# Attention's chunk loop: the state's update is recorded in front of the read-out of the old state

## The chip, the cores and the metric

The program runs on one core of a Trainium2 chip. TensorE (PE, its weight loads are listed apart as PEld), VectorE (DVE), ScalarE (ACT), GpSimd (POOL) and SyncE (SP, which here only starts DMAs) each work through an instruction list of their own and wait for each other through semaphores. The metric is the device time of one execution in microseconds.

## The reference

Three steps follow one another: a recurrent attention, a mixture of eight experts, and a dense layer pair with a squared ReLU. Only the first is touched. For each of 4 x 8 heads a 40 x 40 state is carried over 768 tokens:

```
y[t]  = r[t] . state                                  (read before the update)
Sa    = state . a[t]
state = state * w[t]  -  Sa x b[t]  +  v[t] x k[t]    (outer products)
```

The output of the whole program is `_moe2_ref(_moe_ref(attention))`, 3072 rows of 320 numbers.

## The kernel before

The 768 tokens are cut into 24 chunks of 32. For a chunk the decay is folded into scaled inputs, the 32 x 32 triangular system inside the chunk is inverted, and the state is carried from chunk to chunk in two PSUM tiles, ST0 and ST1. A chunk's work is cut into stages (functions A_... to F_...), and the table ORDER lists the stages of one loop iteration with a lag: `("D_st", 0)` in iteration i works on chunk i, `("E_yi", -1)` on chunk i-1, `("D_R", 1)` on chunk i+1. The loop runs over i = 1 to 21 (`for i in range(1, nch - 2)`); HEAD and TAIL are tables for the chunks before and after. Nothing reorders the work later: within `tc.manual_schedule()` every engine's list is what the stages issue, in the table's order, so each engine's order follows from the table.

Stages that matter here, with their lines:

- E_yi (L732): 16 matmuls that read the old state out for chunk i-1, `y = r . Ss`, where Ss is a transposed copy of the state in SBUF made an iteration earlier. They take a fresh buffer of the PSUM pool psm, which has six buffers in turn.
- D_st (L659, L676): 32 short matmuls add chunk i's contribution to ST0 and ST1, and four ACT copies bring the new state into SBUF (sT). At a window's end (i = 11 inside the loop) DVE rescales the state on the way (L674), followed by filler matmuls (DMY, L328) and matmuls that put the rescaled state back into ST (L682).
- D_R (L622, L629): the right-hand side of chunk i+1. Its first part (L622) needs no state; its second part (L629) reads sT, the copies that D_st of the same iteration has just made.
- E_scm (L723, DVE) masks a score matrix; E_y (L743, PE) multiplies it and adds to the y that E_yi began; E_xs (L771, DVE), the first DVE work of the next iteration, reads the finished y.
- C_inv, C_dn, C_x1, F_2, B_ev and the two scans (L752 and L446) fill DVE's list between L771 and the next L723. B_ev (L509, L513) reads the PSUM tile LM that PE fills at L500.
- loadE, loadL and loadV, loadZ of the next iteration are DMAs that SP starts in this order. loadL (L435, L439) refills xL, the tile whose first part E_yi reads as r, so SP holds it until E_yi is done.

The trace shows each fp32 matmul of the code as two records: the 16 matmuls of E_yi are "x32", the 32 of D_st are "x64".

```
P.matmul(y[32*b : 32*b+32, 2*hp : 2*hp+2], s["r"][:, hp*4+b], s["Ss"][:, hp*4+b], start=(hp == 0), stop=False, ...)   # E_yi, L732
P.matmul(ST[bl][64*hh : 64*hh+40, o : o+40], s["kS"][:, bl, hp, bh, hh], z[:, bh, hp, 40*hh : 40*hh+40], ...)         # D_st, L659
S_.activation(dst, src, AF.Copy)                                                                                     # D_st, L676
P.matmul(R[32*hp : 32*hp+32, b], s["at"][:, hp*4+b], cur[0:NP, hp*4+b], start=False, stop=True, ...)                  # D_R, L629
```

Of the kernel before, what the change touches and what calls it, by code (L numbers as in the profile page):

```python
# [72 lines left out]
def layout(r, k, v, w, a, b, moe_w_gate, moe_w_output_gate, moe_w1, moe_w2, moe2_w_in, moe2_w_out):  # L73
# [65 lines left out]
    ("loadZ", 1),  # L139
    ("B_kt", 2, 1),  # L140
    ("F_3", -2),
    ("E_yi", -1),
    ("loadE", 4),
    ("D_st", 0),
    ("E_W", 0),
    ("A_bd", 3),
    ("loadL", 1),
# [1381 lines left out]
```

## Time and profile before

| | |
|---|---|
| median of 3 runs | 1040.94 us (1035.12 to 1048.4) |
| the profiled execution | 1040.41 us, span 1038.6 us |
| busy in the span | PE 944.7 us (91%), DVE 683.0 (66%), ACT 610.8 (59%), POOL 463.6 (45%) |
| attention's loop | about 78 to 402 us of the span |
| experts and dense layers | about 440 to 1038 us |
| TensorE's granted clock, mean | 0.964 of full speed |

Times within the trace count from the span's start. A row of the timeline gives the start, the length and the number of instructions of a merged group; in brackets stands how long the engine had been idle before it and what ended the wait. "issue" is idle time in which the engine waited for nothing that the profile shows. A row of the waits gives the engine and line that waited, the one waited for, the total in us, the number of times and the longest.

### The profile page before, as it was taken

Reading aid. Unit: us, or ns where it says so; the run is one execution under the profiler, and the core shown is the slowest. Engines: PE = TensorE matmul, PEld = TensorE weight load, DVE = VectorE, ACT = ScalarE, POOL = GpSimd, SP = SyncE. Lnnn points to the kernel's source line nnn. Section 1 sums busy time; section 2 is a strip of 40 time slices with the busy share of each in tenths; the row PEclk is TensorE's granted clock in tenths of the full one; section 3 lists DMA queues with packets and bytes.
Section 4 is the critical chain, followed back from the end, with each engine's and each line's share of the span. In section 5 each row is a group of like instructions: output and inputs, shape, how many; then the busy total and the mean of one; then the engine's idle time right before and its main releaser. Section 6 shows DMA issues by size and latency. Waiting matters only on the chain.

```text
span 1038.6 us, 33215 instructions
## 1 busy us (share of the span) xinstructions
PE 944.7 (91%) x13882; PEld 835.9 (80%) x13882; DVE 683.0 (66%) x1752; ACT 610.8 (59%) x1366; POOL 463.6 (45%) x449
## 2 busy tenths in 40 slices
PE   1779889888889988889999999989999999999997
PEld 1568777777777776789999999978899998889986
DVE  5878899889988986537777777565443343434341
ACT  3569799896888987635555555544434344333432
POOL 5655777776676872527666666520100101010101
PEclk9779999999999999779999999999999999999999
DMA  4873445434344534356888876762001010000000
GB/s 100 247 206 107 114 107 138 124 108 115 107 116 109 144 91 116 111 207 193 246 245 252 245 231 199 214 139 64 29 13 32 26 31 27 1 26 1 17 10 26
DMA packets 59314, 120.33 MB, mean 116 GB/s; under 512 B 14609, under 2 KB 32145, under 8 KB 57233
## 3 DMA queue, kind: packets, MB, share of 16 engines
q1 hardware_dynamic: 51424, 103.09, 35.9%
q0 software_dynamic: 2688, 8.88, 2.4%
q10 hardware_dynamic: 5040, 6.12, 1.7%
q8 instruction: 112, 1.84, 0.8%
q14 instruction: 50, 0.40, 0.1%
HBM read 92.01 MB, written 26.05 MB: 114 GB/s over the span
## 4 chain that ended last, share of the span: by engine, by line
PE 51%; DMA 2%; DVE 1%; issue 1%; ACT 0%; POOLq 0%; POOL 0%; ACTq 0%; DVEq 0%; SPq 0%
PE ph L1226 26%; PE py L1409 9%; PE po L1230 5%; PE po L1229 5%; PE po L1231 5%; PE pk L1276 1%; DMA out_dram<-o,TID 1%; DMA q<-in_wo_dram 1%; DMA yTD<-yT 1%; DMA xg<-yTD 0%; DVE c L1211 0%; DVE c L1194 0%; PE py L1318 0%; POOLq L1524 0%; ACT r L1454 0%
## 5 line engine op out<-in xcount | busy, mean ns | idle before, releaser
L1226 PE MATMUL ph<-x,ring 128*128 128x512 f32 (+2 forms) x1344 | 308.1, 378 | 4.5 <-ACT r L1454 4.5
L1226 PEld LDWEIGHTS ph<-x,ring 128*128 128x128 f32 x1344 | 240.2, 189 | 38.6 <-ACT r L1454 5.0
L1480 POOL DMA_INDIRECT out_dram<-o,TID x24 | 27.9, 1163 | 323.4 <-ACT o L1478 279.5
L1455 DVE TENSOR_TENSOR q<-r 128x512 f32<-128x512 f32 x96 | 66.4, 691 | 122.5 <-ACT r L1454 122.5
L921 POOL TENSOR_TENSOR ring<-raws,ring 128x732 fp32r<-128x732 f32 (+2 forms) x72 | 123.3, 1726 | 48.1 <-ACT ring L920 28.1
L1454 ACT ACTIVATE r<-ph 128x512 f32<-128x512 f32 x96 | 57.3, 597 | 124.4 <-PE ph L1226 124.4
L486 POOL TENSOR_TENSOR arena<-arena 40x1024 f32<-40x1024 f32 x43 | 105.5, 2453 | 37.6 <-DVE arena L468 13.3
L1229 PE MATMUL po<-ring,hh 128*128 128x320 f32 x368 | 114.2, 310 | 0.0
L1230 PE MATMUL po<-ring,hl 128*128 128x320 f32 x368 | 114.1, 310 | 0.0
L1231 PE MATMUL po<-ring,hh 128*128 128x320 f32 x368 | 113.9, 309 | 0.0
L1409 PE MATMUL py<-hw,ring 128*128 128x448 f32 x512 | 106.1, 367 | 0.0
L1457 DVE TENSOR_TENSOR hl<-q,hh 128x512 fp32r<-128x512 f32 x92 | 63.8, 693 | 64.1 <-ACT hh L1456 64.1
L1409 PEld LDWEIGHTS py<-hw,ring 128*128 128x128 f32 x512 | 95.5, 188 | 7.9
L1456 ACT ACTIVATE hh<-q 128x512 fp32r<-128x512 f32 x92 | 58.1, 632 | 70.1 <-DVE q L1455 70.1
L1304 DVE SCALAR_TENSOR_TENSOR hw<-ph,hw 128x448 fp32r<-128x448 f32 (+2 forms) x72 | 41.0, 570 | 51.6 <-ACT hw L1303 51.6
L1229 PEld LDWEIGHTS po<-ring,hh 128*128 128x128 f32 x368 | 69.6, 189 | 4.3
L1230 PEld LDWEIGHTS po<-ring,hl 128*128 128x128 f32 x368 | 69.4, 189 | 3.9
L1231 PEld LDWEIGHTS po<-ring,hh 128*128 128x128 f32 x368 | 69.3, 188 | 0.0
L920 ACT ACTIVATE ring<-raws 128x732 fp32r<-128x732 f32 (+2 forms) x72 | 56.8, 790 | 4.8 <-DMA raws<-in_we_dram 4.2
L1303 ACT ACTIVATE hw<-ph 128x448 fp32r<-128x448 f32 (+2 forms) x72 | 36.1, 501 | 38.0 <-PE ph L1226 37.7
L1198 POOL TENSOR_TENSOR c<-c,r 128x384 int32<-128x384 int32 (+1 forms) x32 | 35.1, 1098 | 49.5 <-ACT yT L1414 12.0
L676 ACT ACTIVATE sT<-ST 40x320 f32<-40x320 f32 x88 | 33.2, 425 | 34.3 <-PE ST L659 34.1
(214 smaller groups left out, 1982.8 us busy)
## 6 DMA issues: line engine op xcount, KB each, us to landing
raws<-in_we_dram SPq DMA_DIRECT2D x48, 366.0 KB
arena<-in_xE_dram SPq DMA_DIRECT2D x48, 322.5 KB
xL<-in_xL_dram SPq DMA_DIRECT2D x24, 480.0 KB
xsD<-raws SPq DMA_DIRECT2D x24, 268.0 KB
q<-in_wi_dram SPq DMA_DIRECT2D x16, 384.0 KB
xg<-xsD SPq DMA_DIRECT2D x7, 804.0 KB
q<-in_wo_dram SPq DMA_DIRECT2D x16, 320.0 KB
wb<-in_wB_dram SPq DMA_DIRECT2D x24, 165.0 KB
```

The costliest lines, as they stand in the source:

```text
L486: (V if c < EARLY[2 + hh] else G).tensor_tensor(out=bd[sl, :, :, hh].rearrange("p a b c l j->p (a b) c (l j)"), in0=s["bk"][sl].rearrange( ...
L920: S_.activation(hi, rw, AF.Copy)
L921: G.tensor_tensor(out=lo, in0=rw, in1=hi.bitcast(F32), op=ALU.subtract)
L1226: P.matmul(ps, t[:, o : o + 128], x3[:, i, c], start=(j == 0), stop=(j == 7))
L1229: P.matmul(ps, hh, whi[:, o : o + 320], start=start, stop=False)
L1230: P.matmul(ps, hl, whi[:, o : o + 320], start=False, stop=False)
L1231: P.matmul(ps, hh, wlo[:, o : o + 320], start=False, stop=stop)
L1409: P.matmul(py, w, x, start=(f == 0 and k == 0), stop=last)
L1454: S_.activation(r, ph, AF.Relu)
L1455: V.tensor_tensor(out=q, in0=r, in1=r, op=ALU.mult)
L1456: S_.activation(hh, q, AF.Copy)
L1457: V.tensor_tensor(out=hl, in0=q, in1=hh.bitcast(F32), op=ALU.subtract)
```

## The change

In ORDER the row of E_yi moves behind the row of D_st. loadE (DMAs on SP) stood between them. HEAD and TAIL stay as they are.

```
--- before.py
+++ after.py
@@ -139,9 +139,9 @@
     ("loadZ", 1),
     ("B_kt", 2, 1),
     ("F_3", -2),
-    ("E_yi", -1),
     ("loadE", 4),
     ("D_st", 0),
+    ("E_yi", -1),
     ("E_W", 0),
     ("A_bd", 3),
     ("loadL", 1),
```

E_yi issues only matmuls, and in iteration 1 it issues none (chunk 0 has no old state), so the move shows in PE's list of 20 iterations; the lists of DVE, ACT, POOL and SP are the same in both kernels.

The first place is PE's list where the two stages stand, before, from the ranking matmul of the router (L895, tile rk) to the first update matmuls:

```order
L895 MATMUL rk<-oh,cnt 128x8 [waits DVE_49,PE_49,Activation_49]
L895 MATMUL rk<-oh,cnt 128x8
L732 MATMUL y<-Ss,xL_111 32x80 [waits DVE_49,PE_49]
L732 MATMUL y<-Ss,xL_111 32x80 x15
L659 MATMUL ST_108<-zS_117,kSB_121 40x40 [waits DMAHW2_49]
L659 MATMUL ST_108<-zS_117,kSB_121 40x40
L659 MATMUL ST_109<-zS_117,kSB_121 40x40 x2
```

The same place of an iteration in the changed kernel, from the last update matmuls to the right-hand side R:

```order
L659 MATMUL ST_108<-zS_118,kSB_124 40x40 x2
L659 MATMUL ST_109<-zS_118,kSB_124 40x40 x2
L732 MATMUL y<-Ss,xL_110 32x80 [waits DVE_49,PE_49]
L732 MATMUL y<-Ss,xL_110 32x80 x15
L622 MATMUL R<-vBD_119,MTm 32x4x40 [waits DMAHW6_49,DMAHW1_49,DMAHW7_49,DMAHW0_49,Activation_49]
L622 MATMUL R<-vBD_119,MTm 32x4x40 x7
L629 MATMUL R<-sT_115,at 32x80 [waits Activation_49]
L629 MATMUL R<-sT_115,at 32x80 x3
```

The update now follows L895 directly, and the read-out, with the wait for its buffer, stands between the update and R. L629's wait for ACT (the copies of the new state) is unchanged.

The second place is SP's list, which is the same in both kernels; it is shown for what loadL (xL, wb) waits for and what stands behind it:

```order
L416 DMA arena<-in_xE_dram 40x2064 [waits DMAHW2_49,Pool_49]
L435 DMA xL_110<-in_xL_dram 80x1536 [waits DMAHW3_49,PE_49]
L439 DMA wb<-in_wB_dram 128x330 [waits DMAHW4_49,DVE_49,Activation_49]
L423 DMA vBD_120<-in_vN_dram 32x320 [waits DMAHW5_49]
L423 DMA vBD_120<-in_vN_dram 32x320 [waits DMAHW6_49]
```

The row of xL waits for PE, and that is for the read-out E_yi, which now ends later in PE's list than before; wb and the four transfers of vBD stand behind it.

## Rows read from the trace of the kernel before

**Rows 1.** Busy time by stretch: length, then each engine, granted clock, DMA share, GB/s.

```profile
core 0: us, PE busy (x) PEld busy (x) DVE busy (x) ACT busy (x) POOL busy (x), PEclk, DMA share, GB/s
100.00:200.00 100.00, 88.12 (x2814) 74.46 (x2812) 89.78 (x307) 85.98 (x224) 72.47 (x80) 0.98 0.45 119
```

**Rows 2.** Waits from 85 to 405 us: who waited, for whom, total, times, longest.

```profile
DVE xs L771 <- PE y L743: 21.8, 17, 3.1
...
PE R L629 <- ACT sT L676: 10.0, 19, 0.7
...
PE y L743 <- issue: 7.6, 13, 2.1
PE y L732 <- DVE arena L513: 7.1, 10, 1.2
```

**Rows 3.** Timeline of PE in iteration 7: start, length, instructions, idle before.

```profile
168.81 0.36 PE L895 MATMUL rk<-oh,cnt 128*128 128x8 f32 x2
169.76 0.76 PE L732 MATMUL y<-Ss,xL 80*32 80x80 f32 x32 [0.58 <-DVE arena L513]
170.45 1.43 PE L659 MATMUL ST<-zS,kSB 128*40 128x40 f32 x64
171.80 0.75 PE L622 MATMUL R<-vBD,MTm 128*32 128x160 f32 x16
173.09 0.95 PE L629 MATMUL R<-sT,at 104*32 104x80 f32 x32 [0.54 <-ACT sT L676]
173.85 0.32 PE L743 MATMUL y<-kSB,scm 128*32 128x40 f32 x13
174.34 0.73 PE L743 MATMUL y<-kSB,scm 128*32 128x40 f32 x51 [0.17 <-issue]
```

**Rows 4.** Timeline of DVE in the same iteration.

```profile
168.94 0.67 DVE L513 STREAM_TRANSPOSE arena<-LM 128x512 f32<-128x512 f32 x1
...
172.46 0.67 DVE L723 TENSOR_TENSOR scm<-sc,cst 128x512 f32<-128x512 f32 x1
173.06 1.28 DVE L446 TENSOR_TENSOR_SCAN Cx<-arena 104x528 f32<-104x528 f32 x1
175.11 0.49 DVE L771 TENSOR_TENSOR xs<-y,WN 128x320 f32<-128x320 f32 x1 [0.77 <-PE y L743]
```

**Rows 5.** Timeline of ACT in the same iteration.

```profile
169.58 0.94 ACT L546 ACTIVATE kSB<-kt,cst 128x320 f32<-128x320 f32 x2
171.84 1.52 ACT L676 ACTIVATE sT<-ST 40x320 f32<-40x320 f32 x4 [1.33 <-PE ST L659]
```

**Rows 6.** DVE's groups by line, 85 to 405 us: busy, mean ns, idle before.

```profile
L771 DVE TENSOR_TENSOR xs<-y,WN 128x320 f32<-128x320 f32 x20 | 9.8, 488 | 22.8 <-PE y L743 21.8 <-PE tp L696 1.0
```

**Rows 7.** DVE at the window's end, iteration 11.

```profile
234.89 1.80 DVE L674 TENSOR_TENSOR sT<-ST,cw 40x320 f32<-40x320 f32 x4 [1.03 <-PE ST L659]
```

**Rows 8.** Timeline of PE at the window's end, iteration 11.

```profile
240.98 0.80 PE L743 MATMUL y<-kSB,scm 128*32 128x40 f32 x64 [0.78 <-DVE dB L765]
```

**Rows 9.** Waits of SP's queue, 85 to 405 us.

```profile
SPq L435 <- PE y L732: 127.5, 20, 8.5
```

**Rows 10.** PE's unexplained idle in E_y, iteration 15.

```profile
308.66 0.42 PE L743 MATMUL y<-kSB,scm 128*32 128x40 f32 x24 [2.12 <-issue]
```

**Rows 11.** DMA queue that carries instructions: packets, MB, share.

```profile
q8 instruction: 112, 1.84, 0.8%
```

**Rows 12.** PE's unexplained idle behind E_y, iteration 8.

```profile
192.47 0.60 PE L706 MATMUL zt<-cst,zS 128*80 128x128 f32 x4 [1.20 <-issue]
```

**Rows 13.** DVE afterwards, in iteration 9's first half.

```profile
197.63 0.16 DVE L876 TENSOR_REDUCE mx<-xs 128x1 f32<-128x8 f32 x1 [0.73 <-ACT xs L874]
...
198.99 1.25 DVE L509 STREAM_TRANSPOSE LB<-LM 128x1024 f32<-128x1024 f32 x1 [0.39 <-PE LM L500]
```

**Rows 14.** Busy time by stretch behind the loop, columns as in rows 1.

```profile
470.00:650.00 180.00, 180.00 (x929) 165.92 (x928) 137.18 (x260) 100.73 (x205) 116.68 (x80) 1.00 0.78 229
650.00:685.00 35.00, 30.47 (x146) 27.07 (x145) 21.87 (x41) 16.68 (x33) 20.86 (x14) 1.00 0.68 180
```

More of the change, by code (lines that the diff above doesn't have):

```diff
@@ L141 @@
     ("F_3", -2),
-    ("E_yi", -1),
     ("loadE", 4),
     ("D_st", 0),
+    ("E_yi", -1),
     ("E_W", 0),
```

## The prediction

> **What bounds the kernel now.** I read the busy times by stretch first. In attention's loop PE is busy 88% of the time, DVE 90%, ACT 86% [rows 1]: no engine is full, two run nearly level, so an iteration is set by where these two wait for each other. The waits of the loop show where. DVE's largest wait for PE is at L771, the first work on a finished y: 21.8 us in 17 iterations [rows 2], and with one more releaser 22.8 us over 20 iterations, about 1.1 us each [rows 6]. PE's two semaphore waits in the stretch that ends with that y are L629 for the copies of the new state (10.0 us, 19 times) and L732 for its buffer (7.1 us, 10 times) [rows 2]. The timelines of iteration 7 put them in one line: L732 starts 0.58 us late because DVE's L513 must first release a buffer, then come the update (L659), R's first part (L622), 0.54 us of waiting for ACT's copies, L629 and E_y (L743) [rows 3]; DVE has then been idle 0.77 us when it starts L771 at 175.11 [rows 4].
>
> **The change part by part.** Nothing is added or removed: 20 read-outs and 20 updates swap places on PE. The four ACT copies (L676) don't move in ACT's list, nor does SP's list change.
>
> *The wait for the copies.* The update now follows L895, which ends at 168.81 + 0.36 = 169.17 [rows 3]. It takes 1.43 us, so it ends at 170.6 instead of 171.88. ACT must be free then: its previous work L546 ends at 169.58 + 0.94 = 170.52 [rows 5], and it has idled 1.33 us before L676 in this iteration, so it is. L629 started 1.21 us behind the end of the update (173.09 against 171.88) and so may start at 171.8. On PE the read-out (0.69 us to the next start) and L622 (0.75 us) now stand between and end at 172.0. They cover the copies with 0.2 us to spare; the 0.54 us go.
>
> *The wait for the buffer.* L513 ends at 169.61 [rows 4], while the update runs; the read-out now asks for the buffer at 170.5. Those 0.58 us go as well.
>
> *What is late next.* L629 would be through at 172.7, but E_y needs L723's mask, which DVE ends at 172.46 + 0.67 = 173.13 [rows 4]. E_y starts there instead of at 173.85: 0.7 us won. It ends at 174.35, and DVE's L446 ends at 173.06 + 1.28 = 174.34, so L771 finds its input at once. In such an iteration the two engines meet, and 0.7 us is all there is.
>
> *The sum.* Of the 10 iterations with the buffer wait one is the window's end; the other 9 have both waits: 9 x 0.7 = 6.3 us. The 10 others have the wait for the copies alone, 0.54 us; in one of them DVE does not wait for PE (18 of 20 do [rows 2, 6], and the other exception is the window's end): 9 x 0.54 = 4.9 us. At the window's end DVE waits 1.03 us for the update itself [rows 7], and the update comes about as much earlier; the read-out then stands behind the rescaling, where its 0.7 us fit into the 0.78 us that E_y waits for DVE anyway [rows 8]: 1.0 us. Together 12.2 us. The largest it could be is DVE's whole waiting, 22.8 + 1.0 = 23.8 us.
>
> *What may be given back.* E_y also holds 7.6 us of idle in 13 pieces that no semaphore explains [rows 2], up to 2.12 us [rows 10]. There is a queue that carries only instructions, 112 packets of 16 KB [rows 11]; I take these pieces to be PE waiting for its own instructions. If such a piece ends at the same moment however early PE arrives, 0.54 us are lost there: at most 13 x 0.54 = 7.0 us, at least nothing. Most pieces are short (0.17 us in iteration 7 [rows 3], the mean is 0.58), so I take back 2 us, nearer the lower end. The Trainium skill ("Runtime: NRT & Kernel Launch", section "Instruction fetch mechanics") says instructions come in blocks of 16 KiB and that crossing into the next is mostly hidden; by that the sum would stay 12.2. The packet size agrees [rows 11]; "hidden" does not fit the 2.12 us [rows 10], if they are what I take them for.
>
> *SP.* loadL waits for the read-out 20 times [rows 9]. It now starts later by the update's 1.35 us (170.45 to 171.80 [rows 3]) less the buffer wait, and wb and vBD behind it too. They serve the next chunk, whose first use of them is a whole iteration away, and I cost the delay itself at nothing.
>
> *Behind the loop* PE is busy 100% of the 180 us from 470 on, and the 35 us behind them hang on work that PE releases [rows 14]. A shorter loop should shift all of it.
>
> 12.2 - 2 = 10.2 us off the profiled execution's 1040.41 gives **1030.2 us**. The median of the runs is 0.5 us above that execution, which I leave out.
>
> **Rivals.**
>
> *Nothing is given back.* For it: the short pieces may not be instruction waits at all. 1040.4 - 12.2 = 1028.2 us. The rule of the Trainium skill named above ("Runtime: NRT & Kernel Launch", "Instruction fetch mechanics") would give this time.
>
> *PE is held by its instructions.* For it: from L895 to the end of E_y there are 210 matmul records in 6.3 us [rows 3], and the unexplained idle sits at their end. All 13 pieces grow by what is won: 12.2 - 7.0 = 5.2 us, 1035.2 us; if iterations that have no such piece get one, or the 35 us behind the loop are set by DMA, it goes to no gain, 1040.
>
> *The idle in E_y goes too.* The xL transfer, which starts where the read-out ends, now starts nearer to E_y's end; if instruction packets have queued behind it during the update, they no longer do. 12.2 + 7.6 = 19.8 us, 1020.6 us.
>
> *Slower.* The same transfers (xL, wb, vBD) now run beside R, E_y and the transposes behind it, and the instruction wait moves there. It is not free: 1.20 us of it in iteration 8 [rows 12] was followed by DVE waits of 0.73 and 0.39 us [rows 13], 1.12 us in all. A gain of 0.6 us per iteration is eaten once each iteration gets 0.7 us of new idle there. At 1.20 us in all 20: 20 x 1.12 - 12.2 = 10 us slower, 1050.6 us; at 2.12 us about 1069. Against it: DMA is busy only 45% in the loop [rows 1].
>
> That the move does nothing (the update waiting for z or kS where the read-out stood) would need a wait that L659 never shows among the loop's waits although it starts at most about 1 us earlier; I count it into the no-gain end.
>
> **How the numbers follow.** Chances: the forecast (1026 to 1034) 0.45, nothing given back 0.13, held by instructions 0.20, the idle goes too 0.10, slower 0.12. The range 1020 to 1041 leaves out half of the tenth and most of the slower case. A change of 2%, 20.8 us, is about what a measurement of this kernel can tell from none. Below 1020.1 lies only the part of the fourth case in which nearly all of DVE's waiting goes: 0.05. Above 1061.8 only the slower case with the longest idle everywhere: 0.02. Within 2%: 0.93.
>
> **What would show it.** In the profile of the changed kernel L629's wait for ACT and L732's for L513 should be gone or near zero, and L743 should wait for DVE instead, 0.2 to 0.5 us per iteration. L771's 22.8 us should fall to about 12. From one L771 to the next it should be about 0.5 us less on average. If L743's unexplained idle is larger than 7.6 us, PE is held by its instructions; if it moved to L706, L696 or L607 and DVE waits more at L876 and L509, the transfers moved it. The prediction is wrong if L629 still waits, if the loop shortens without the end moving, or if the loop gets longer.

## The result and the profile after

The changed kernel takes **1029.17 us** (median of 6 runs, 1026.09 to 1034.66) beside 1040.93 us of the kernel before in the same series (6 runs, 1035.12 to 1048.4). The ratio is **0.990, 95% interval 0.986 to 0.994**. Run again, as the first of the experiments, it gave 0.994 (0.990 to 0.998). Ratios leave out executions more than 1.5% above the fastest of their kernel, so they can differ from the ratio of the medians. The prediction was 1030.2 us, and the medians came within 1 us of it.

The profiled execution of the change is the slowest of its six, 1034.66 us (span 1032.9). Its waits in attention's loop, 83 to 402 us, columns as in [rows 2]:

```profile
DVE xs L771 <- PE y L743: 8.3, 7, 2.3
...
PE y L743 <- issue: 5.4, 6, 1.6
...
DVE mx L876 <- ACT xs L874: 4.9, 5, 2.0
...
PE y L743 <- DVE scm L723: 3.6, 8, 0.8
```

PE's wait at L629 for the copies (10.0 us before) and L732's for DVE's L513 (7.1 us) have no row left. L743 waits for the mask instead, as was expected. Iteration 7 on PE, DVE and ACT, beside [rows 3 to 5]:

```profile
170.11 0.36 PE L895 MATMUL rk<-oh,cnt 128*128 128x8 f32 x2
170.41 1.43 PE L659 MATMUL ST<-zS,kSB 128*40 128x40 f32 x64
171.76 0.76 PE L732 MATMUL y<-Ss,xL 80*32 80x80 f32 x32
172.34 0.73 PE L622 MATMUL R<-vBD,MTm 128*32 128x160 f32 x16
173.05 0.94 PE L629 MATMUL R<-sT,at 104*32 104x80 f32 x32
174.38 1.09 PE L743 MATMUL y<-kSB,scm 128*32 128x40 f32 x64 [0.39 <-DVE scm L723]
```

```profile
173.65 0.68 DVE L723 TENSOR_TENSOR scm<-sc,cst 128x512 f32<-128x512 f32 x1
174.24 1.28 DVE L446 TENSOR_TENSOR_SCAN Cx<-arena 104x528 f32<-104x528 f32 x1
175.52 0.49 DVE L771 TENSOR_TENSOR xs<-y,WN 128x320 f32<-128x320 f32 x1
```

```profile
171.80 1.52 ACT L676 ACTIVATE sT<-ST 40x320 f32<-40x320 f32 x4
```

The first copy starts as the update ends, and L629 follows L622 without a wait: read-out and L622 cover the copies. E_y waits 0.39 us for the mask, and DVE goes from L446 to L771 without idling. From L895's start to E_y's end it is 5.36 us instead of 6.26. DVE's groups, 83 to 402 us, at L771 and at the window's end (beside [rows 6, 7]):

```profile
L771 DVE TENSOR_TENSOR xs<-y,WN 128x320 f32<-128x320 f32 x20 | 9.5, 475 | 8.4 <-PE y L743 8.3
...
L674 DVE TENSOR_TENSOR sT<-ST,cw 40x320 f32<-40x320 f32 x4 | 1.8, 484 | 0.0
```

L771's idle fell from 22.8 to 8.4 us, and L674's 1.03 us are gone. The whole loop, from the first L771 (iteration 1) to the 21st, columns as in [rows 1]: the kernel before, the change, and the second execution of the change (1028.12 us):

```profile
78.77:401.78 323.01, 288.99 (x9061) 245.60 (x9061) 287.57 (x983) 274.94 (x710) 227.50 (x256) 0.98 0.43 114
```

```profile
76.36:394.06 317.70, 289.81 (x9061) 248.87 (x9062) 294.53 (x983) 276.82 (x710) 229.03 (x256) 0.97 0.43 114
```

```profile
76.42:387.52 311.10, 285.24 (x9061) 244.04 (x9061) 289.67 (x984) 278.57 (x712) 228.60 (x256) 1.00 0.44 117
```

DVE's busy time is 287.57, 294.53 and 289.67 us. Its idle time (length less busy) goes from 35.4 to 23.2 and 21.4 us. But its busy time, for the same work, rises by 7.0 and 2.1 us, so the loop is only 5.3 and 11.9 us shorter. Where DVE's own time grows is the first open question; the second is why the two executions differ by 6.6 us. Outside the loop two differences nearly cancel. Its first L771 starts 2.4 us earlier than before (76.36 and 76.42 us instead of 78.77), where the lists are still the same, so that is not the change's. From the 21st L771 to the end it takes 638.8 us in both instead of 636.8.

DVE's groups for two small instructions of the router, 76 to 402 us, first before, then the change:

```profile
L878 DVE SCALAR_TENSOR_TENSOR val<-xs,mx,cst 128x8 f32<-128x8 f32 x20 | 8.3, 413 | 0.7
...
L882 DVE TENSOR_SCALAR oh<-val,mv 128x8 fp32r<-128x8 f32 x20 | 5.9, 295 | 0.7
```

```profile
L882 DVE TENSOR_SCALAR oh<-val,mv 128x8 fp32r<-128x8 f32 x20 | 12.2, 611 | 0.7
...
L878 DVE SCALAR_TENSOR_TENSOR val<-xs,mx,cst 128x8 f32<-128x8 f32 x20 | 10.8, 538 | 0.7
```

Together 14.2 us before and 23.0 after. One iteration of the change, DVE and then POOL:

```profile
182.16 0.59 DVE L878 SCALAR_TENSOR_TENSOR val<-xs,mx,cst 128x8 f32<-128x8 f32 x1
182.78 0.16 DVE L880 TENSOR_REDUCE mv<-val 128x1 f32<-128x8 f32 x1
182.98 1.05 DVE L882 TENSOR_SCALAR oh<-val,mv 128x8 fp32r<-128x8 f32 x1
```

```profile
180.36 2.36 POOL L486 TENSOR_TENSOR arena<-arena 40x1024 f32<-40x1024 f32 x1 [2.65 <-DVE ST L570]
182.80 1.20 POOL L473 TENSOR_TENSOR at<-arena,Cx 104x512 f32<-104x512 f32 x1
183.96 1.18 POOL L463 TENSOR_TENSOR arena<-Cx,arena 104x512 f32<-104x512 f32 x1
```

L878 ends when POOL's L486 does, and L882, 0.23 us elsewhere, ends when L473 does. L882 takes over 0.5 us 2 times in 20 before and 11 times in this execution of the change: a DVE that arrives earlier meets POOL's products.

### The profile page after: what moved, and what is told of

It is laid out like the page before. It is cut to its first block, busy times and chain, and to the rows that moved or that the text cites. A ratio compares the mean times of both kernels' runs of the same rounds, so it can differ in the third digit from the quotient of the medians.

```text
span 1032.9 us, 33234 instructions
## 1 busy us (share of the span) xinstructions
PE 945.0 (91%) x13882; PEld 838.3 (81%) x13882; DVE 688.8 (67%) x1752; ACT 611.9 (59%) x1366; POOL 465.9 (45%) x449
## 4 chain that ended last, share of the span: by engine, by line
PE 52%; DMA 2%; DVE 1%; issue 1%; ACT 0%; POOL 0%; SPq 0%; POOLq 0%; ACTq 0%; DVEq 0%
PE ph L1226 26%; PE py L1409 9%; PE po L1230 5%; PE po L1229 5%; PE po L1231 5%; PE pk L1276 1%; DMA yTD<-yT 1%; DMA raws<-wiD 0%; DMA raws<-woD 0%; DVE c L1211 0%; DMA out_dram<-o,TID 0%; POOL ring L921 0%; PE py L1318 0%; ACT ring L920 0%; DVE c L1194 0%
## 5 line engine op out<-in xcount | busy, mean ns | idle before, releaser
L1226 PE MATMUL ph<-x,ring 128*128 128x512 f32 (+2 forms) x1344 | 308.9, 378 | 4.6 <-ACT r L1454 4.6
L1226 PEld LDWEIGHTS ph<-x,ring 128*128 128x128 f32 x1344 | 240.6, 190 | 39.0 <-ACT r L1454 5.0
L921 POOL TENSOR_TENSOR ring<-raws,ring 128x732 fp32r<-128x732 f32 (+2 forms) x72 | 123.1, 1722 | 52.5 <-ACT ring L920 26.5
L486 POOL TENSOR_TENSOR arena<-arena 40x1024 f32<-40x1024 f32 x43 | 106.4, 2475 | 42.2 <-DVE arena L468 12.5
L546 ACT ACTIVATE kSB<-kt,cst 128x320 f32<-128x320 f32 x96 | 45.0, 520 | 15.3 <-PE kt L543 15.1
```

The lines of the kernel that those rows point to most:

```text
L486: (V if c < EARLY[2 + hh] else G).tensor_tensor(out=bd[sl, :, :, hh].rearrange("p a b c l j->p (a b) c (l j)"), in0=s["bk"][sl].rearrange( ...
L921: G.tensor_tensor(out=lo, in0=rw, in1=hi.bitcast(F32), op=ALU.subtract)
L1226: P.matmul(ps, t[:, o : o + 128], x3[:, i, c], start=(j == 0), stop=(j == 7))
```

## The experiments

Ratios are to the kernel before on the same chip, with their 95% interval.

**The change again**, for a second profile.

> The changed kernel once more, beside the others of this set, to have its ratio to the kernel before on the same chip. The theory (PE's waits for the copies of the state and for the read-out's buffer are hidden, DVE's mask is the next limit) and its rivals all expect the ratio seen so far, 0.986 to 0.994, about 1030 us.

1029.71 us, ratio 0.994 (0.990 to 0.998): the gain is there again, 0.6% this time. This execution had no half-clock stretch in the loop (clock 1.00 above). Its waits, 83 to 400 us:

```profile
DVE xs L771 <- PE y L743: 15.8, 18, 2.1
...
PE y L743 <- DVE scm L723: 5.9, 9, 1.0
```

**Half of the read-out on either side of the update.**

```
-    ("loadE", 4), ("D_st", 0), ("E_yi", -1),
+    ("E_yi", -1, 0), ("loadE", 4), ("D_st", 0), ("E_yi", -1, 1),   # hp 0,1 / hp 2,3
```

> Half of the read-out's matmuls stay in front of the update, half go behind it. The first half still asks for the buffer, so the 7.1 us of buffer waits stay; the second half (0.35 us) and R's first part (0.75 us) cover 1.1 of the 1.21 us that the copies take. Theory: some 0.43 us in 19 iterations, 5 to 8 us, ratio 0.992 to 0.995, L629's wait for ACT falls from 10.0 to about 2 us and L732's for L513 stays near 7. Rival, the buffer wait alone paid: ratio 1.00. Rival, the later start of the xL transfers paid: most of the gain comes here too, since the second half holds xL as long as in the change.

Ratio 0.998 (0.995 to 1.002): a miss. The waits, 85 to 400 us:

```profile
PE y L732 <- DVE arena L513: 7.3, 11, 1.2
...
PE R L629 <- ACT sT L676: 3.3, 13, 0.3
```

The copies' wait fell by 6.7 us, as meant, but L771's, over the same 20 iterations, by 3.6 only, from 21.8 to 18.2. L878 and L882 took 22.5 us, 8.3 more than before, and the loop had 20 us at half clock instead of 12; which of the two took the gain isn't shown. A ratio of 1.00 is also what the rival "the buffer wait alone paid" expected, and L732's wait is still there (7.3 us). "The later start of the xL transfers paid" expected most of the gain here, and that did not come.

**The read-out behind R.**

```
-    ("E_yi", -1), ("E_W", 0), ("A_bd", 3), ("loadL", 1), ("E_rng", 0), ("D_R", 1),
+    ("E_W", 0), ("A_bd", 3), ("E_rng", 0), ("D_R", 1), ("E_yi", -1), ("loadL", 1),
```

> The read-out (and loadL, which must follow it) goes behind the whole of R. The update covers the buffer wait as in the change, but nothing new covers the copies: L629 should wait for ACT about 0.5 us in 19 iterations again, L732 not at all. Theory: what is left is the buffer wait in 9 iterations, 4 to 6 us, ratio 0.994 to 0.997. Rival, the copies alone paid: ratio 1.00. Rival, the later transfers matter: xL now starts another 1.5 us later than in the change and the ratio moves away from the theory's, below 0.992 or above 1.00.

Ratio 1.007 (1.003 to 1.012): a miss on the wrong side, as the rival "the later transfers matter" had it. The profile is of an execution of 1055.21 us, at a mean clock of 0.949. In it L732's wait for L513 is gone and L629 still waits 6.8 us for the copies, as expected, and PE has 6.1 us of unexplained idle at L715, where before had none; that the later loadL brought it is likely, not shown. The version moves a transfer besides the read-out, so it does not price the buffer wait alone; nothing here does.

**The mask in front of the scan CB.** E_y's wait for L723 was to go as well.

```
+    ("E_scm", -1),
     ("E_W", 0),
     ...
-    ("E_scm", -1),
```

> The changed kernel with DVE's mask (L723) in front of E_W's scan and transpose instead of behind them, so that it is ready about 1.6 us earlier. Theory: in the change L743 waits for DVE (3.6 us for L723, 1.4 for the line that came last at the window's end); that wait goes, PE gains up to 5 us more, while DVE's list keeps its length: ratio 0.984 to 0.988, L743 no longer waits for DVE. Rival, PE is held by its instructions: the unexplained idle of L743 grows by as much and the ratio stays at 0.990. Rival, DVE's own list is the limit: the ratio stays at 0.990 and L771 waits no longer.

Ratio 1.022 (1.016 to 1.027): far off. L771 hardly waits any more (0.8 us), yet the loop is longer. DVE and POOL in one iteration:

```profile
172.25 1.42 DVE L752 TENSOR_TENSOR_SCAN CB<-wb,dB 128x330 f32<-128x330 f32 x1
173.71 0.75 DVE L758 STREAM_TRANSPOSE WN<-CB 128x320 f32<-128x320 f32 x1
174.30 3.76 DVE L446 TENSOR_TENSOR_SCAN Cx<-arena 104x528 f32<-104x528 f32 x1
```

```profile
171.70 1.27 POOL L534 TENSOR_TENSOR MTm<-arena,cst 128x512 f32<-128x512 f32 x1
173.13 1.41 POOL L905 DMA_INDIRECT xsD<-xs,POS  x1 [0.15 <-issue]
174.57 2.37 POOL L486 TENSOR_TENSOR arena<-arena 40x1024 f32<-40x1024 f32 x1
```

The scan L446 takes 3.76 us instead of 1.28: 2.48 more, for POOL's 2.37, and it ends 1.12 us behind L486. Its mean over the loop was 3706 ns. L752 (0.83 in the change) starts behind L534 and loses 0.6.

**POOL's list in another order**, on the change, on the kernel before and on the version with the early mask. L473 now needs the finished scan and comes first, the other products follow it, and the scatter (L905) comes last:

```
     ("A_scan", 3),
+    ("A_at", 3), ("A_bd", 2),      # were behind E_sc, and ("A_bd", 3) behind E_W
     ...
-    ("A_recip", 3),
+    ("A_recip", 3), ("F_4", -3),   # F_4: the scatter of F_3, an iteration later
```

HEAD leaves its last A_bd to the loop, and TAIL begins with the scatter that is left.

> The change, and GpSimd's list in another order: the product at (L473) waits behind the scan L446 and comes first, both halves of the product bd (L486) follow, then L463, and the scatter of the routed rows (L905) last. Theory: in the change GpSimd's 1.2 us products L473 and L463 hold up VectorE's L878 and L882 (0.23 us alone, 0.8 to 0.9 us beside them; 6 to 9 us in the loop), and that is where a part of the gain is given back. Here both products are done before L878 starts, so L878 and L882 should take 0.23 us each in nearly all 20 iterations, no scan L446 should be longer than 1.4 us, and the time should be 6 to 10 us below the change: ratio to the kernel before 0.983 to 0.989. Rival: the two stretched instructions lie beside a wait for PE anyway, so their 0.23 us return but the time is that of the change, 0.991 to 0.997.

> GpSimd's order as in the other kernel of this call, on the kernel before (read-out in front of the update). By the theory that the change itself brings VectorE's L878 and L882 under GpSimd's products, the kernel before has little of it (2 long L882 of 20, 3 long scans L446): 2 to 7 us faster, ratio 0.993 to 0.998. By the rival (GpSimd's order is worth the same whatever stands around it, and has nothing to do with the change) the ratio is as far below 1 as the other kernel is below the change, 0.990 or less if that gains, 1.000 if that doesn't.

> The change with GpSimd's new order, and the mask L723 in front of the scan L752, as in the kernel that lost 2% to the one before. By the theory that this loss came from GpSimd's L486 running before and beside the scan L446 (3.7 us instead of 1.28), L446 is 1.28 us again since GpSimd's list now waits for it, E_y (L743) no longer waits for the mask, and the time is at or below the change: ratio 0.978 to 0.990. If the early mask itself costs (the scan L752 and the transposes behind it come later, for whoever waits for them), the loss stays: 1.01 to 1.03.

On the change 0.987 (0.982 to 0.993), on the kernel before 1.002 (0.998 to 1.007), on the early mask **0.990 (0.986 to 0.993)**. DVE's groups, 76 to 402 us: the change with POOL's new order, then the early mask with it, then the early mask without.

```profile
L446 DVE TENSOR_TENSOR_SCAN Cx<-arena 104x528 f32<-104x528 f32 x18 | 22.2, 1232 | 0.0
...
L878 DVE SCALAR_TENSOR_TENSOR val<-xs,mx,cst 128x8 f32<-128x8 f32 x21 | 7.6, 362 | 0.7
...
L882 DVE TENSOR_SCALAR oh<-val,mv 128x8 fp32r<-128x8 f32 x21 | 5.2, 250 | 0.8
```

```profile
L446 DVE TENSOR_TENSOR_SCAN Cx<-arena 104x528 f32<-104x528 f32 x18 | 21.5, 1196 | 0.0
```

```profile
L446 DVE TENSOR_TENSOR_SCAN Cx<-arena 104x528 f32<-104x528 f32 x18 | 66.7, 3706 | 0.0
```

With the mask in the same early place and POOL's products kept off the scan, the loss of 2.2% turns into a gain of 1.0%; the intervals lie far apart. That POOL's products stretch DVE's scan, and that this made the loss, is shown. On the change itself L878 and L882 fall to 12.8 us (about 10 was expected), and DVE's busy time in the loop to 278.9 us:

```profile
78.60:388.43 309.83, 283.79 (x9061) 241.50 (x9062) 278.90 (x984) 275.85 (x709) 227.40 (x256) 0.99 0.45 117
```

But the time falls only 3 to 6 thousandths below the two series of the change, and the intervals overlap: this gain is likely, not shown. The row says why it is small. Beside the second execution of the change, whose clock was nearly the same, DVE is busy 10.8 us less and idle 9.5 us more (30.9 instead of 21.4), and the loop is only 1.3 us shorter: most of the stretched time lay where DVE would have waited for PE anyway, as the rival had it. On the kernel before POOL's order gains nothing (2 to 7 thousandths were expected). The difference between the two gains is within the noise, so that it is worth the same on both isn't excluded.

**The part r of xL in a tile of its own**, with three buffers, so that loadL does not wait for the read-out.

```
-        nc.sync.dma_start(out=x, in_=A["xL"][c])
+        nc.sync.dma_start(out=x, in_=A["xL"][c][:, 512:1536])
+        nc.sync.dma_start(out=xr[c % 3], in_=A["xL"][c][:, 0:512])
```

> The change, with the part r of xL (what the read-out uses) in a tile of its own with three buffers: SP's loadL then no longer waits for the read-out, and the transfers of xL and wb start some 3 to 8 us earlier in an iteration; one DMA more per chunk. If PE's unexplained idle inside E_y (10.2 us in the loop in one execution of the change) is a wait for instruction packets that queue behind these transfers, it falls below 5 us and the time by 3 to 8 us: ratio 0.986 to 0.991. If it is not tied to these transfers, it stays at 5 to 10 us and the time with the change, 0.991 to 0.997.

Ratio 1.015 (1.010 to 1.021): neither. PE's unexplained idle did not stay or shrink, it moved and grew. First the second execution of the change, then this kernel, 80 to 400 us:

```profile
PE y L743 <- issue: 10.2, 24, 0.7
...
PE x L600 <- issue: 1.9, 4, 0.8
...
PE ST L659 <- issue: 1.7, 3, 0.8
```

```profile
PE ST L659 <- issue: 13.5, 6, 3.5
...
PE x L600 <- issue: 7.0, 5, 2.6
...
PE y L732 <- issue: 5.7, 4, 2.8
...
PE y L743 <- issue: 5.5, 5, 1.6
...
PE kt L543 <- issue: 5.4, 2, 4.1
```

16.5 us in all lines became 40.5, in fewer and longer pieces, at other lines. The trace's records of the instruction queue fit. I took the places inside one line's run of weight loads, 78 to 400 us, where the next load starts over 0.9 us after the one before, in five executions (the kernel before, the change twice, the version with filler matmuls below, and this one). All 61 end 1.1 to 1.8 us after an instruction packet has landed, where 14 to 18% of all weight loads start; 22 of them are here and 5 in the change's second execution. Within each execution they also stand a whole multiple of about 126.5 weight loads apart, to within 8 loads, which is close to the 126 to 128 loads per packet in that stretch. So the long pieces are PE waiting for instructions. This version has more and longer ones; whether that comes from the place of the xL transfer or from the one transfer more isn't separated. Of the pieces between 0.5 and 0.9 us in that second execution only 12 of 25 end so; what the others are stays open.

**The mask further forward** (in front of B_ev), without and with POOL's new order.

> The change, with the mask L723 three places further forward than in the version that lost 2%: in front of the transposes L509 and L513 instead of in front of the scan L752. From L509 to L446 VectorE's list is then 0.67 us shorter, and GpSimd's list hangs on L509. Theory (the 2% were the scan L446 standing behind GpSimd's L486): L446 starts 0.7 us earlier against L486 and stays at 1.28 us, E_y (L743) no longer waits for L723, and DVE's wait at L771 (15.8 us in one execution of the change) falls by 3 to 6 us: ratio to the kernel before 0.986 to 0.992. If an early mask costs by itself, wherever it stands (everything behind it in DVE's list comes 0.67 us later), the ratio is 1.00 or more.

> The same place of the mask together with GpSimd's new order (both products of VectorE's busy time out of the way of L878 and L882). If the two savings add, L752 stays near 0.9 us (it took 1.4 us where the mask stood right in front of it), L882 at 0.23 and L446 at 1.24 us: ratio 0.978 to 0.987, below each of the two alone. If PE or ACT sets the iteration by then, it is no better than GpSimd's order alone, 0.985 to 0.991.

0.998 (0.993 to 1.002) without, **0.986 (0.982 to 0.990)** with it, 1023.81 us. The first missed the 0.986 to 0.992 of its theory, but does not refute it: L446 took 1.55 us in most iterations and up to 3.97, so the mask's place did not keep it clear of POOL. The second is the lowest of all versions and beats the kernel before; its interval overlaps that of POOL's order alone, so that the savings add isn't shown.

**Half a move with POOL's new order.**

> Half of the read-out in front of the update and half behind it, with GpSimd's new order. The half move alone gave 0.998 where 0.992 to 0.995 was expected. Theory: it brought 8.5 us of stretched L878 and L882 as the whole move did, but only half of its gain; with GpSimd's products out of the way both are 0.23 us, and the ratio is 0.988 to 0.994. If the half move gains nothing because the buffer wait (L732 for L513, 7 us) is still there and hides what the copies' wait gave, it stays at 0.995 to 1.001.

Ratio 0.998 (0.994 to 1.002): the theory missed. L878 and L882 fell to 10.7 us, yet the ratio did not move. The other reason that was named, the buffer wait, does not fit the one profile (1025.56 us, the fastest of its twelve): L732's wait for L513 is gone there, and L629 waits 4.5 us. Brought to equal clock (6.4 us per 0.01 of mean clock, the slope within the series of the kernel before, for the runs that the ratios use), this version lies 2.7 us below the kernel before (95%: 0.7 to 4.7) and half a move alone 0.3 us below (1.9 above to 2.5 below). Both are short of the 6 to 12 us that the theory expected here. Why half a move gains so little stays open.

**Packet ends moved**: 32 two-column filler matmuls before PE's first work.

```
 HEAD = [
-    ("A_scan", 0),
+    ("warm", 0, 32, 2), ("A_scan", 0),
```

> The change, with 32 filler matmuls of two columns (64 records) in front of PE's first work, while PE is idle for the program's first 19 us. They cost nothing themselves; they move every later instruction of PE by half of the 129 weight loads that one instruction packet holds, so the ends of the packets fall on other places of the iterations. Theory A: a part of what the change gained is only where these ends fall (PE's waits for instructions, and the stretches at half clock that follow the long ones): then the unexplained idle stands at other lines and iterations than in the change, the mean clock over the runs is 0.957 to 0.966 instead of 0.969, and the ratio to the kernel before is 0.996 to 1.005. Theory B: the gain is that of the two waits that went, wherever the packets end: clock 0.966 to 0.972, ratio 0.989 to 0.996. In both L629's wait for ACT and L732's for L513 stay gone.

Ratio 0.989 (0.985 to 0.993), median of the clock 0.967: theory B. The unexplained idle stood elsewhere (L743 6.3 us, L600 4.7, L659 3.8, L696 3.5) and the gain stayed: in this one other placing it does not hang on where the instruction packets end. By the spacing above a packet holds about 126.5 weight loads, not 129; the shift is half of that all the same. The profiled execution shows the gain of the loop less well: the loop is 319.58 us, 3.4 less than before, with 27.2 us of unexplained idle, and the rest of the 11.9 us stands ahead of the loop (5.2) and behind it (3.3).

## Why the prediction was right, step by step

The waits that were to go went; the size was met in part by luck.

*The wait for the copies* and *the wait for the buffer*: right. Both rows are gone, in both executions.

*What is late next*: right. L743 waits for DVE's mask, 3.6 us in 8 iterations and 5.9 in 9, 0.45 and 0.66 us each (0.2 to 0.5 was expected). That DVE is then level with PE holds for one execution: in iteration 7 L771 follows L446 directly, and L771 waits in 7 of 20 iterations. In the second it still waits in 18 of 20, 15.8 us, and L743 holds 24 short pieces of unexplained idle in it. Freeing E_y from the mask (the early mask with POOL's order) brought no more than POOL's order alone.

*The sum of 12.2 us*: DVE's idle time fell by 12.2 and 14.0 us, and L771's 22.8 us to 8.4 and 15.8, where about 12 was expected. But idle time that longer instructions fill is not time won. With POOL's new order, where they are short again, DVE idles 30.9 us, only 4.5 less than before. As a gain in time the sum was too large: at equal clock about 7 us of the 10.2 came, as is shown below. How that divides between the two waits no run shows.

*What may be given back*: incomplete. The 2 us were put on PE's instruction waits. The long pieces of that idle are such waits, and all of it rose from 13.6 us before to 19.4 and 16.5 in PE's rows of 80 to 400 us. Another item was not in the prediction: 8.8 us more in L878 and L882, because DVE now reaches them while POOL's products run. The prediction took DVE's durations from the rows of before, as if they were DVE's own; they depend on what POOL does at that moment. What these 8.8 us cost is less. Brought to equal clock as above, the change lies 6.3 us below the kernel before in its second series and 8.4 with the fillers, and POOL's order on it 9.6, each about 2 us either way: some 1 to 3 us, within the noise. That in the second execution the loop still fell by 11.9 us goes with a shorter scan L446 (26.5 us instead of 31.3 in the stretch from 76 us) and with the clock.

*The clock* is the other thing the sum did not hold. The loop of before had 12 us at half clock in this execution, the change's 17 and 0. Over all runs the mean granted clock has a median of 0.963 before (88 runs) and 0.969 in the change (18 runs). Among runs of equal clock (0.962 to 0.966) the medians are 1039.2 (34 runs) and 1032.1 us (5), at 0.967 to 0.971 they are 1035.8 (18) and 1029.0 (8). So about 7 us go with the change at equal clock, and the remaining 3 to 5 with the higher clock. Whether the change raises the clock or these runs happened to have it is open. The forecast of 10.2 us was thus met by 7 us and 3 that it had not named; that the time came so close is luck as far as those 3 go.

*SP* and *behind the loop*: right in the main. loadL's wait for the read-out rose from 127.5 to 148.7 us (134.3 in the second execution) with no harm seen. From the first expert work (L1226) to the end it takes 584.1 us before and 584.4 after; of the loop's gain 1 to 2 us are lost between its end and that work.

*The rivals.* "Nothing is given back" (1028.2) lies within the runs' spread and can't be told from the forecast by the time; PE's and DVE's rows speak against it. The rule behind it is that fetching is mostly hidden (the Trainium skill, "Runtime: NRT & Kernel Launch", section "Instruction fetch mechanics"). By count the trace agrees in the change's second execution, where 5 of some 70 packets in the loop are followed by a gap of over 0.9 us; with the moved xL it is 22 of 66, and a wait reaches 4.1 us. "PE is held by its instructions" had L743's unexplained idle above 7.6 us as its sign: it is 5.4 in one execution and 10.2 in the other, so a part of it may be at work. "The idle in E_y goes too" did not come. "Slower" rested on transfers beside instruction waits. Its sign, more waiting of DVE at L876 and L509, is there in one execution (4.9 and 2.5 us after 2.9 and 1.9) and not in the other (1.6 and none). The moved xL shows that such waits can grow, but its 1.5% also hold 48 us at half clock and a longer scan L446 (mean 2089 ns instead of 1649).

## What to carry to other kernels

When a wait goes, its engine runs earlier against every other engine: look at what then overlaps, above all DVE's scans and two-input instructions beside POOL's elementwise work, and order POOL's list by a dependence that keeps them apart. Take an instruction's price from its shortest row and ask of the longer ones what ran beside them, and whether they only fill time in which their engine would have waited. And read a gain of 1% at equal clock, since the runs of one kernel differ by as much.

## What the runs showed of the hardware

**Some DVE instructions wait out a POOL product beside them.** L446 1.28 to 3.76 us beside a 2.37 us product, L752 0.83 to 1.42, L882 0.23 to 1.05. It can also be POOL that pays: its L534 takes 1.27 us where it starts ahead of the scan L752 and 1.87 where it starts 0.05 us behind it. The Trainium skill ("SBUF — State Buffer", section "Who interferes with whom") says that an instruction of DVE with two SBUF inputs, or in a two-port mode, contends with GpSimd for a shared port pair, and that the order of issue decides who blocks. The trace agrees that one waits for the whole of the other; the transposes and the mask with one input in PSUM (L723) kept their lengths. The order can't be read from the recorded starts alone: L446's row starts 0.27 us ahead of L486's in the early mask, and L446 waits. For L882, which reads one tensor and one column of numbers, no run shows which of the two cases it is.

**Half clock mostly follows idle.** Of the 46 stretches at half clock that begin between the first and the 21st L771 of the 14 profiled executions, 41 begin less than 2.5 us behind the end of a gap of PE of over 1 us, or inside it; of the 141 such gaps 100 are followed by none. In the profile after, busy time by stretch before, in and behind a gap at L715 (1.41 us):

```profile
88.00:94.00 6.00, 5.83 (x168) 4.30 (x160) 5.97 (x24) 5.91 (x17) 5.79 (x3) 1.00 0.78 189
94.10:95.40 1.30, 0.01 (x2) 0.01 (x2) 1.30 (x5) 1.27 (x5) 0.00 (x0) 1.00 0.47 90
96.10:109.70 13.60, 13.60 (x260) 12.07 (x254) 9.24 (x21) 7.38 (x18) 9.32 (x13) 0.50 0.17 44
```

The granted clock (third number from the right) is 1.00, then 0.50 (1.2 GHz) for 13.6 us, and this iteration, the gap included, took 21.9 us where the loop's median is 15.4. After the 1.42 us at L743 in iteration 11 the clock stayed at 1.00. Over the 88 runs of the kernel before, 0.01 less of mean clock goes with about 7.8 us more.
